# Sums of one pair issued ahead of the masks of the next in quarter-array blocks, with an earlier A, an earlier O unit and a split weight load

## The chip, the cores and the metric

The kernel runs on one core of a Trainium2 chip (trn2). The metric is the device time of one execution in microseconds (us); the span in a profile is 1 to 2 us shorter, because it goes from the first to the last instruction.

Engine names: PE is TensorE (matmuls), PEld its weight loads, DVE is VectorE, ACT ScalarE, POOL GpSimd, SP SyncE. L316 is a line of the kernel. The changed kernel is seven lines longer from the state update on, so L388, L418, L442 of the kernel before are L395, L425, L449 after, and the mask line L352 is L351.

## The reference

Linear attention with a decaying state (batch 4, 8 heads, 768 steps, head size 64), then a feed-forward layer whose activation is h·cos(h):

```python
for t in range(S):
    state = gamma * state + k[t] v[t]^T          # per batch and head
    y[t] = (1/sqrt(D)) * q[t] @ state
x = y, heads joined                               # 3072 x 512
h = x @ w_in                                      # 512 -> 2048
out = (h * cos(h)) @ w_out                        # 2048 -> 512
```

The kernel works on chunks. A "pair" is two batches of one chunk of 128 steps; there are twelve pairs, and two pairs form a group of 512 tokens. Per pair: **A** = keys times queries, **masks** (DVE, lower triangle), **sums** = masked A times values, **Y** = the state's part of y, **U** = the state update. **F** is a piece of the first feed-forward matmul, followed by a cosine on ACT and a product on DVE; **O** is a quarter of a 128-token tile of the second.

## The kernel before: the parts that matter

From pair 4 on, Y, A, U and the sums run as 64x64 matmuls, four at a time in quarters of the PE array. One block holds Y of pair p, A and U of pair p+1, then the masks of p+1, then the sums of p. Sums and A results share four PSUM banks: sums in columns 0-255, A in columns 256-511.

```python
def block(py=None, pa=None, pu=None, split=False):
    yb = {(u, r): banks.take() for u in range(2) for r in range(2)}
    ...                                   # Y of py -> yb[..][:, :256]; A of pa -> yb[..][:, 256:]
    ...                                   # U of pu -> two more banks
    if py is not None and not split:
        order = nc.sync.nop(nofuse=True)  # SP passes on that A has ended
        tc.add_manual_dep(order.ins, last.ins.name, SYNC, reason="sums in order")
    if pa is not None:
        for b in range(2):
            for r in range(2):
                masked = nc.vector.tensor_tensor(out=am[pa % 2][r][:, b],
                    in0=yb[b, r][:, 256:]..., in1=mask..., op=ALU.mult)
                order = order or masked
    def sums():
        ...                               # 32 matmuls into yb[u, b][:, :256], b outermost
        ...                               # four ACT copies of yb[u, b][:, :256] into xt
        ...                               # give the four banks back
    ...
    elif not split:
        sums()                            # with split, the caller issues them one slot later
```

The start, where the first weights come in, and the stretch between the early and the steady stage:

```python
load(nc.gpsimd, 1, ("q0", "k0", "q1", "k1"))
load_w_in(0)                              # columns 0-511, 1 MB in HBM
load(nc.gpsimd, 1, ("v0", "v1"))
...
m1 = stage_a(1, (0,)); masks(1, m1)
later = []
pair_f(0, 0, (0,), later)                 # first F: needs columns 0-255
m1 = stage_a(1, (1,)); masks(1, m1)
conv_v_plain(1, 0); conv_v_plain(1, 1)    # ACT
pair_f(0, 0, (1,), later)
...
stage_y(1, nc.scalar.copy)
...
pair_f(1, 0)                              # first F of pair 1: needs both xt copies
...
plan[1] = [(0, "c", 5), (1, "t", 4), (3, "a", 4), (4, "c", 6), (6, "t", 5), (8, "B", 4),
           (10, "c", 7), (13, "Y", 5)]    # (slot, what, pair): c casts and loads, t transposes
for g in range(1, NG + 1):
    for s in range(16):
        if 1 < g < NG: unit_f(g, s)
        unit_o(g - 1, *divmod(s, 4))
        ...                               # then what the plan has for slot s
```

Of the kernel before, what the change touches and what calls it, by code (L numbers as in the profile page):

```python
# [31 lines left out]
def kernel(  # L32
# [9 lines left out]
    nc = tc.nc  # L42
# [82 lines left out]
    def load_w_in(r, n=512):  # L125
        nc.gpsimd.dma_start(
            out=w_in_sb[:, :, ts(r, n)],
            in_=moe_w_in[:, ts(r, n)].rearrange("(i p) f -> p i f", p=128))
# [95 lines left out]
    def stage_a(p, bs=(0, 1)):  # L224
        n = p % NB
        todo = []
        for b in bs:
            bk = [banks.take(), banks.take()]
            ap = [t.rearrange("p (a t) -> p a t", a=HP) for t in bk]
            for a in range(HP):  # L230
                for j in range(2):
                    po = 64 * j
                    nc.tensor.matmul(ap[j][:, a, :], lhsT=kt(n, b, a)[po : po + 64, :],  # L233
                                     rhs=qt(n, b, a)[po : po + 64, :],
                                     tile_position=(po, 0))
            todo.append((b, bk, ap))
        return todo
# [67 lines left out]
    def block(py=None, pa=None, pu=None, split=False):  # L305


        started = set()
        yb = {}
        if py is not None or pa is not None:  # L310
            yb = {(u, r): banks.take() for u in range(2) for r in range(2)}

        def mm(bank, col, cols, row, lhsT, rhs):
            first = (id(bank), col) not in started
            started.add((id(bank), col))
            return nc.tensor.matmul(bank[half(col), cols], lhsT=lhsT, rhs=rhs, start=first,  # L316
                                    stop=True, skip_group_check=True,
                                    tile_position=(64 * row, 64 * col))

        if py is not None:  # L320
            n = py % NB
            for a in range(HP):
                for u in range(1 if py % NC == 0 else 0, 2):
                    st = stb[py % 2][:, 0] if u == 1 else stb[(py - 1) % 2][:, 1]
                    for b in range(2):
                        for i in range(2):
                            mm(yb[u, b], i ^ b, ts(a, 64), i, st[half(i), ts(4 * b + a, 64)],
                               qt(n, b, a)[half(i), half(u)])
        if pa is not None:
            n = pa % NB  # L330
            for b, a in BA:
                for u in range(2):
                    for i in range(2):
                        last = mm(yb[b, i ^ u], u, ts(4 + a, 64), i,
                                  kt(n, b, a)[half(i), half(u)], qt(n, b, a)[half(i), half(u)])
        ub = []
        if pu is not None:
            n = pu % NB
            ub = [banks.take() for _ in range(1 if pu % NC == NC - 1 else 2)]
            for b, a in BA:  # L340
                for i in range(2):
                    for u, bank in enumerate(ub):
                        mm(bank, i, ts(4 * b + a, 64), u, ks[n][half(u), b, 2 * a + i, :],
                           vs[n][half(u), b, 2 * a + (i ^ b), :])
        order = None
        if py is not None and not split:
            order = nc.sync.nop(nofuse=True)
            tc.add_manual_dep(order.ins, last.ins.name, SYNC, reason="sums in order")
        if pa is not None:
            for b in range(2):  # L350
                for r in range(2):  # L351
                    masked = nc.vector.tensor_tensor(  # L352
                        out=am[pa % 2][r][:, b],
                        in0=yb[b, r][:, 256:].rearrange("p (a t) -> p a t", a=HP),
                        in1=mask.unsqueeze(1).to_broadcast([128, HP, 64]), op=ALU.mult)
                    order = order or masked

        def sums():
            n = py % NB
            if order is None:  # L360
                nc.tensor.drain()
            for b, a in BA:
                for j in range(2):
                    for u in range(2):
                        m = mm(yb[u, b], j, ts(a, 64), u, vs[n][half(u), b, 2 * a + j, :],
                               am[py % 2][j ^ b ^ u][half(u), b, a, :])
                        if order is not None and b == a == j == u == 0:
                            tc.add_manual_dep(m.ins, order.ins.name, SYNC, reason="sums in order")
            for b in range(2):
                for u in range(2):  # L370
                    nc.scalar.copy(  # L371
                        out=xt[(py // 2) % 2].rearrange(
                            "p a (h b u t) -> p h b u a t", h=2, b=2, u=2)[:, py % 2, b, u],
                        in_=yb[u, b][:, :256].rearrange("p (a t) -> p a t", a=HP))
            for bank in yb.values():
                banks.give(bank)

        if py is None:
            for bank in yb.values():
                banks.give(bank)  # L380
        elif not split:
            sums()
        if pu is not None:
            for u, bank in enumerate(ub):
                if pu % NC == 0 and u == 0:
                    nc.vector.tensor_copy(out=stf[:, 0], in_=bank)
                else:
                    nc.vector.tensor_tensor(out=stf[:, u], in0=bank, in1=stf[:, 1 - u],  # L388
                                            op=ALU.add)
                banks.give(bank)  # L390
                nc.scalar.copy(out=stb[pu % 2][:, u], in_=stf[:, u])  # L391
        return sums
# [29 lines left out]
    def pair_f(p, r, parts=(0, 1), later=None):  # L422

        g, hf = divmod(p, 2)
        for f in [4 * r + 2 * i for i in parts]:  # L425
            bank = banks.take()
            for e in range(2):
                for i in range(KIN):
                    nc.tensor.matmul(bank[:, ts(e, 256)], lhsT=w_in_sb[:, i, ts(f + e, 128)],  # L429
                                     rhs=xt[g % 2][:, i, ts(hf, 256)],  # L430
                                     start=(i == 0 and e == 0), stop=(i == KIN - 1),
                                     skip_group_check=True)
            act(bank, gt[g % 2][:, f : f + 2, ts(hf, 256)], later)
# [33 lines left out]
    def masks(p, items):  # L467
        for it in items:
            stage_m(p, it)

    load(nc.gpsimd, 1, ("q0", "k0", "q1", "k1"))
    load_w_in(0)
    load(nc.gpsimd, 1, ("v0", "v1"))
    conv_q(1, nc.gpsimd, (1,))
    load_w_in(1)
# [30 lines left out]
    stage_t(1, None, (1,))  # L506
    m1 = stage_a(1, (0,))
    masks(1, m1)
    later = []
    pair_f(0, 0, (0,), later)  # L510
    m1 = stage_a(1, (1,))
    masks(1, m1)
    conv_v_plain(1, 0)
    conv_v_plain(1, 1)
    pair_f(0, 0, (1,), later)
# [38 lines left out]
    masks(3, m3)  # L554
    pair_f(2, 2, (1,))
    pair_f(2, 3, (0,))
    stage_y(3, nc.scalar.copy)
    pair_f(2, 3, (1,))
    pair_f(3, 0)
    pair_f(3, 1)  # L560
    conv_k(4)
# [13 lines left out]
    sums = None  # L575
    for g in range(1, NG + 1):
        for s in range(16):
            if 1 < g < NG:
                unit_f(g, s)
            unit_o(g - 1, *divmod(s, 4))  # L580
            if sums is not None:
                sums()
                sums = None
            for at, what, p in plan.get(g, ()):
                if at != s or p >= NP:
                    continue
                if what == "t":
                    stage_t(p, False)
                elif what == "c":
                    if p > 5:  # L590
                        conv_q(p, nc.vector if g == 1 else nc.gpsimd)
                    conv_k(p)
                    if p >= PT:
                        stage_t_dma(p)
                    conv_v(p, nc.gpsimd)
                    if p + 2 < NP:
                        load(nc.sync, p + 2, ("q", "v0"))
                        load(nc.gpsimd, p + 2, ("k", "v1"))
                elif what == "a":
                    block(pa=p, pu=p)  # L600
                elif what == "b":
                    block(py=p, pa=p + 1, pu=p + 1)
                elif what == "B":
                    sums = block(py=p, pa=p + 1, pu=p + 1, split=True)
                else:
                    sums = block(py=p, split=True)
# [30 lines left out]
```

## Time and profile before

Three runs gave 222.04, 222.47 and 226.68 us. PE is the limit: it is busy 93% of the span, so I expected that only its idle time could be won (the result shows that this was too narrow). These lines are from the page of the kernel before: the span, PE's busy time, the granted PE clock in 40 slices (tenths of full speed), and the group of the 27 masks that read a plain bank (busy us, mean ns, then idle of DVE before them).

```profile
span 220.0 us, 5315 instructions
...
PE 204.7 (93%) x2214; PEld 112.8 (51%) x2236; DVE 112.5 (51%) x194; ACT 125.4 (57%) x218; POOL 83.2 (38%) x93
...
PEclk9996999999999999999999999999999999999998
...
L352 DVE TENSOR_TENSOR am<-bank,mask 128x256 bf16<-128x256 f32 x27 | 9.9, 415 | 3.3 <-PE bank L316 3.3
```

The clock row is full except in one slice (16.5 to 22 us) and in the last, after the last matmul. The next fence is the time line of one block, at 121 us (start, duration, engine, line, operation, count; the U matmuls are left out).

```profile
121.07 0.44 PE L316 MATMUL bank<-qkt,stb 64*64 64x64 bf16 x32
...
121.34 0.44 PE L316 MATMUL bank<-qkt 64*64 64x64 bf16 x32
...
121.74 1.42 DVE L352 TENSOR_TENSOR am<-bank,mask 128x256 bf16<-128x256 f32 x4
...
122.22 0.19 PE L316 MATMUL bank<-am,vs 64*64 64x64 bf16 x1
...
122.88 0.65 PE L316 MATMUL bank<-am,vs 64*64 64x64 bf16 x31 [0.48 <-DVE am L352]
...
123.07 0.68 DVE L388 TENSOR_TENSOR stf<-bank,stf 128x512 f32<-128x512 f32 x1
123.23 1.20 ACT L371 CAST xt<-bank 128x256 bf16<-128x256 f32 x4 [2.23 <-PE bank L316]
```

A ends at 121.78, the U matmuls at 122.10. The sums (`bank<-am,vs`) start at 122.22 and end at 123.53: the first stands alone, right after the first mask, and the other 31 come 0.66 us later, right after the third mask. The list of waits of PE sums this up as follows (total us, times, longest):

```profile
PE bank L316 <- DVE am L352: 2.4, 6, 0.5
```

At the start PE idles from 15.82 to 17.24 us for the first weights. In the windows below (length, then busy us of PE, PEld, DVE, ACT, POOL, then the clock as a share of full speed, the DMA share and GB/s) PE does nothing from 16 to 17 us, and has half its clock after that:

```profile
16.00:17.00 1.00, 0.00 (x0) 0.00 (x0) 1.00 (x3) 0.45 (x1) 0.89 (x2) 0.95 1.07 215
17.00:18.00 1.00, 0.76 (x4) 0.58 (x5) 0.23 (x1) 0.00 (x0) 0.52 (x1) 0.50 1.19 201
...
19.00:20.00 1.00, 1.00 (x11) 0.63 (x11) 0.22 (x1) 0.77 (x2) 0.14 (x2) 0.50 1.19 193
20.00:21.00 1.00, 0.98 (x8) 0.79 (x7) 1.00 (x3) 0.94 (x2) 0.90 (x1) 0.84 1.27 210
```

### The profile page before, as it was taken

What the parts mean: (1) busy time and instruction counts of PE and PEld (TensorE: products, weight loads), DVE (VectorE), ACT (ScalarE), POOL (GpSimd) and SP (SyncE); (2) the same over time, 40 slices, a digit from 0 to 9 for tenths busy, and PEclk for the clock granted to TensorE, in tenths of its full rate; (3) what the DMA queues carried; (4) which work ended last, traced back from release to release, by engine and by line L of the source; (5) the groups of instructions that cost most, each with busy time, mean ns of one, the idle gap of its engine ahead of it and who ended that gap; (6) DMA issues with size and microseconds to landing.
All of it is one profiled execution on the core that took longest, in us unless ns stands there. A gap on an engine that the chain in (4) does not pass through costs nothing.

```text
span 220.0 us, 5315 instructions
## 1 busy us (share of the span) xinstructions
PE 204.7 (93%) x2214; PEld 112.8 (51%) x2236; DVE 112.5 (51%) x194; ACT 125.4 (57%) x218; POOL 83.2 (38%) x93
## 2 busy tenths in 40 slices
PE   7878999999999999999899899899899999999992
PEld 2445878878755444444544544544444444444440
DVE  4685498697569227654643644544544244433000
ACT  5564887867957644685565565664544644454120
POOL 7995679964999737370703300000000000000000
PEclk9996999999999999999999999999999999999998
DMA  6999999999677999979865531441011011110221
GB/s 157 301 205 221 284 317 240 197 254 344 193 261 168 265 309 203 297 114 258 167 119 170 51 95 48 55 95 48 4 48 48 3 49 48 51 48 0 95 81 62
DMA packets 43256, 32.85 MB, mean 149 GB/s; under 512 B 32480, under 2 KB 36832, under 8 KB 43232
## 3 DMA queue, kind: packets, MB, share of 16 engines
q0 software_dynamic: 8320, 18.35, 32.7%
q1 hardware_dynamic: 34768, 14.03, 27.9%
q8 instruction: 17, 0.28, 0.5%
q10 hardware_dynamic: 144, 0.13, 0.2%
q14 instruction: 7, 0.06, 0.1%
HBM read 27.26 MB, written 6.29 MB: 153 GB/s over the span
## 4 chain that ended last, share of the span: by engine, by line
PE 75%; DVE 8%; ACT 5%; DMA 4%; POOL 3%; issue 3%; DVEq 0%; POOLq 0%
PE bank L442 30%; PE bank L418 21%; PE bank L429 10%; DMA w_in_sb<-in_moe_w_in_dram 4%; PE st_ps L418 4%; PE st_ps L442 3%; PE bank L316 3%; DVE am L352 3%; DVE gt L407 2%; ACT cosb L400 2%; POOL kf L120 1%; DVE am L242 1%; PE bank L203 1%; ACT ks L186 1%; ACT qkt L207 1%
## 5 line engine op out<-in xcount | busy, mean ns | idle before, releaser
L407 DVE TENSOR_TENSOR gt<-bank,cosb 128x512 bf16<-128x512 f32 x86 | 58.0, 689 | 68.5 <-ACT cosb L400 68.5
L442 PE MATMUL bank<-w_out_sb,gt 128*128 128x512 bf16 x345 | 85.4, 379 | 0.7 <-issue 0.5
L400 ACT ACTIVATE cosb<-bank,halfpi 128x512 bf16<-128x512 f32 x86 | 58.2, 690 | 42.1 <-PE bank L418 33.1
L442 PEld LDWEIGHTS <-gt 128*128 128x128 bf16 x384 | 37.1, 98 | 43.6
L418 PE MATMUL bank<-xt,w_in_sb 128*128 128x512 bf16 x210 | 55.1, 379 | 1.1 <-issue 0.6
L418 PEld LDWEIGHTS <-w_in_sb 128*128 128x128 bf16 x256 | 24.4, 98 | 29.0 <-issue 0.5
L429 PE MATMUL bank<-xt,w_in_sb 128*128 128x256 bf16 x248 | 29.9, 279 | 1.9 <-DMA w_in_sb<-in_moe_w_in_dram 1.4
L429 PEld LDWEIGHTS <-w_in_sb 128*128 128x128 bf16 x256 | 25.0, 100 | 5.7 <-DMA w_in_sb<-in_moe_w_in_dram 1.6
L181 POOL TENSOR_TENSOR vs<-vf,gk 128x512 bf16<-128x512 f32 x20 | 21.4, 1093 | 10.8 <-PE bank L316 8.3
L176 POOL TENSOR_TENSOR qs<-qf,gq 128x512 bf16<-128x512 f32 x15 | 15.4, 1044 | 24.5 <-issue 7.4
L454 ACT COPY ob<-bank 128x512 f32<-128x512 f32 x21 | 12.5, 594 | 10.7 <-PE bank L442 10.6
L120 POOL DMA_DIRECT2D vf<-in_v_dram x16 | 15.0, 938 | 3.5 <-DMA w_in_sb<-in_moe_w_in_dram 2.6
L120 POOL DMA_DIRECT2D kf<-in_k_dram x15 | 15.8, 1054 | 1.0 <-DMA w_in_sb<-in_moe_w_in_dram 0.6
L371 ACT CAST xt<-bank 128x256 bf16<-128x256 f32 x28 | 8.7, 383 | 12.8 <-PE bank L316 12.8
L407 DVE TENSOR_TENSOR gt<-st_ps,cosb 128x512 bf16<-128x512 f32 x10 | 6.9, 690 | 10.3 <-ACT cosb L400 10.2
L242 DVE TENSOR_TENSOR am<-bank,mask 128x512 bf16<-128x512 f32 x16 | 10.1, 682 | 3.5 <-PE bank L233 3.5
L391 ACT CAST stb<-stf 128x512 bf16<-128x512 f32 x14 | 8.4, 639 | 5.7 <-DVE stf L388 3.7
L352 DVE TENSOR_TENSOR am<-bank,mask 128x256 bf16<-128x256 f32 x27 | 9.9, 415 | 3.3 <-PE bank L316 3.3
L186 ACT CAST ks<-kf 128x512 bf16<-128x512 f32 x20 | 11.5, 630 | 0.0
L207 ACT COPY qkt<-bank 128x1024 bf16<-128x1024 bf16 x8 | 7.9, 1012 | 5.6 <-PE bank L203 5.6
L400 ACT ACTIVATE cosb<-st_ps,halfpi 128x512 bf16<-128x512 f32 x10 | 6.9, 691 | 7.0 <-PE st_ps L418 6.9
L176 DVE TENSOR_TENSOR qs<-qf,gq 128x512 bf16<-128x512 f32 x9 | 10.0, 1136 | 1.4 <-DMA qf<-in_q_dram 1.4
(69 smaller groups left out, 157.5 us busy)
## 6 DMA issues: line engine op xcount, KB each, us to landing
out_dram<-ob SPq DMA_DIRECT2D x23, 256.0 KB, 2.0
kf<-in_k_dram POOLq DMA_DIRECT2D x8, 512.0 KB, 6.8
vf<-in_v_dram POOLq DMA_DIRECT2D x13, 256.0 KB, 7.0
qf<-in_q_dram SPq DMA_DIRECT2D x5, 512.0 KB, 5.9
w_in_sb<-in_moe_w_in_dram POOLq DMA_DIRECT2D x4, 512.0 KB, 10.1
w_out_sb<-in_moe_w_out_dram POOLq DMA_DIRECT2D x4, 512.0 KB, 9.1
kf<-in_k_dram POOLq DMA_DIRECT2D x7, 256.0 KB, 7.3
qf<-in_q_dram POOLq DMA_DIRECT2D x6, 256.0 KB, 7.6
```

The source lines that it names most:

```text
L120: eng.dma_start(out=t[p % PRE][:, bs].rearrange("p b h d -> p (b h) d"), in_=src[2 * bp : 2 * bp + 2, :, ds(c * C, C)][bs].rearrange("b h ...
L176: eng.tensor_tensor(out=slots(p, qs[p % NB], b), in0=pairs(qf[p % PRE][:, b]), in1=pairs(bc(gq, p % NC)), op=ALU.mult)
L181: eng.tensor_tensor(out=vs[p % NB][:, b], in0=vf[p % PRE][:, b], in1=bc(gk, p % NC), op=ALU.mult)
L186: nc.scalar.copy(out=slots(p, ks[p % NB], b), in_=pairs(kf[p % PRE][:, b]))
L242: nc.vector.tensor_tensor(out=am1[p % 2][b][j], in0=ap[j], in1=mask1.unsqueeze(1).to_broadcast([128, HP, 128]), op=ALU.mult)
L352: masked = nc.vector.tensor_tensor(out=am[pa % 2][r][:, b], in0=yb[b, r][:, 256:].rearrange("p (a t) -> p a t", a=HP), in1=mask.unsqueeze( ...
L400: nc.scalar.activation(out=cb, in_=bank, func=AF.Sin, bias=halfpi)
L407: nc.vector.tensor_tensor(out=out, in0=h, in1=cb, op=ALU.mult)
L418: nc.tensor.matmul(bank, lhsT=w_in_sb[:, i, ts(f, 128)], rhs=xt[g % 2][:, i, :], start=(i == 0), stop=(i == KIN - 1))
L429: nc.tensor.matmul(bank[:, ts(e, 256)], lhsT=w_in_sb[:, i, ts(f + e, 128)], rhs=xt[g % 2][:, i, ts(hf, 256)], start=(i == 0 and e == 0), s ...
L442: nc.tensor.matmul(bank, lhsT=gt[g % 2][:, f, ts(j, 128)], rhs=w_out_sb[:, f, :], start=(f == 0), stop=(f == KOUT - 1))
L454: nc.scalar.copy(out=o, in_=bank)
```

## The change

Its intent is to take waits off PE: sums no longer wait for masks, PE fills its wait for the first weights with A of pair 1, the first weights come in two halves, an F piece and an O unit fill the waits around Y of pair 3, and one of the two copies of transposed data of pairs 4 and 5 goes to DVE.

```diff
@@ block
-        if py is not None and not split:
-            order = nc.sync.nop(nofuse=True)
-            tc.add_manual_dep(order.ins, last.ins.name, SYNC, reason="sums in order")
-        if pa is not None:
+        def masks():
+            first = None
             for b in range(2):
                 for r in range(2):
                     masked = ...
+            return first
...
+        if split:
+            order = masks() if pa is not None else None
+        elif py is not None:
+            order = nc.sync.nop(nofuse=True)
+            tc.add_manual_dep(order.ins, last.ins.name, SYNC, reason="sums in order")
+            sums()
+        if not split:
+            if pa is not None:
+                masks()
             for bank in yb.values():
                 banks.give(bank)
...
@@ start
-    load_w_in(0)
+    load_w_in(0, 256)
+    load_w_in(1, 256)
...
+    m1 = stage_a(1, (1,))
+    masks(1, m1)
     later = []
     pair_f(0, 0, (0,), later)
-    m1 = stage_a(1, (1,))
-    masks(1, m1)
@@ pair 3
     pair_f(2, 3, (0,))
+    pair_f(2, 3, (1,))
     stage_y(3, nc.scalar.copy)
-    pair_f(2, 3, (1,))
+    unit_o(0, 0, 0)
     pair_f(3, 0)
@@ loop
-            unit_o(g - 1, *divmod(s, 4))
+            if (g, s) != (1, 0):
+                unit_o(g - 1, *divmod(s, 4))
...
-                    stage_t(p, False)
+                    stage_t(p, True)
```

More of the change, by code (lines that the diff above doesn't have):

```diff
@@ L355, in block @@
                         in1=mask.unsqueeze(1).to_broadcast([128, HP, 64]), op=ALU.mult)
-                    order = order or masked
+                    first = first or masked
+            return first
         def sums():
@@ L374, in sums @@
                         in_=yb[u, b][:, :256].rearrange("p (a t) -> p a t", a=HP))
+            if split:
+                for bank in yb.values():
+                    banks.give(bank)
+        if split:
+            order = masks() if pa is not None else None
[6 more added lines that the diff above has]
+                masks()
             for bank in yb.values():
                 banks.give(bank)
-        if py is None:
-            for bank in yb.values():
-                banks.give(bank)
-        elif not split:
-            sums()
         if pu is not None:
```

## The prediction

> **What bounds the kernel now.** TensorE: the page shows PE busy 204.7 of 220.0 us (93%), and the chain of waits is 75% PE. The change adds almost no work, so it can only win PE's idle time. By windows: 0-20 us 4.2 us idle, 20-60 us 1.5, 60-80 us 1.1, 80-160 us 4.0, then almost none until the tail.
>
> **Steady stage (largest term).** Five blocks (near 92, 105, 121, 138, 154 us) have sums of one pair and masks of the next. Timeline at 121 us: the U matmuls end at 122.10; the first sum starts at 122.22, after mask 1 (ends 122.16); the second at 122.88, after mask 3 (122.84); sums end 123.53; the next F starts at 123.68. Masks read and sums write the same PSUM banks at other columns. The Trainium skill, "PSUM — Partial Sum Buffer", section "PSUM bank collisions raise a hardware error", says to guard PSUM by bank, not by address; the trace agrees: a sum waits for its bank's mask. With sums first they run from 122.15 to 122.8: 0.7 us a block. At 92 us the first sum waits for SP (93.18), held by an output DMA: 0.5 there. Sum 3.3 us. The masks (1.4 us), state additions and casts come 1 to 2 us later; DVE (51%) and ACT (57%) are not the limit and the results are wanted eight slots (14 us) later, so nothing is given back.
>
> **Start.** PE idles 15.8-17.24 us for the first 512 weight columns; A of pair 1, second half, is ready at 16.04 but queued behind. After: A at 16.1-16.6, the first 256 columns near 16, F from 16.6. The granted clock is 0.5 from 17 to 20.3 us; it may stay higher. But F of pair 1 waits for both xt copies, on ACT behind the v conversions and a cosine, and the second v of pair 1 lands at 19.98. Estimate: conversions end 20.65 instead of 20.95, F at 22.6 instead of 23.14. The extra weight DMA costs POOL 0.77 us of issue. Gain 0.5 us (0 to 1.2).
>
> **Pair 3.** Its Y waits 48.34-48.93 for the last mask. An F piece (0.87 us) ahead covers this; the O unit (0.86 us) covers the xt copies. Gain 0.45 us.
>
> **Pairs 4, 5.** One of two transposed copies moves from ACT (1.0 us) to DVE (0.69). Block 4/5 now waits for ACT until 68.81, gap 0.28 us. Risk: on DVE the copy stands behind the pair 6 q conversions (one took 3.09 us beside POOL's multiplies). Gain 0.3 us (-0.6 to 0.5).
>
> **Predicted time.** Gain about 4.5 us from fast runs near 222.3: 217.9 us, range 216.3 to 220.0. Chances: faster by over 2% 0.50, within 2% 0.48, slower 0.02.
>
> **What would show it.** In the five blocks no wait of sums for masks (now 2.4 us in six waits), masks after sums, first stb matmul to next F 1.9 instead of 2.6 us; slots still 1.73 us. F before 17 us; F of pair 1 at 22-22.8. No idle inside Y of pair 3. Group 2's first F near 76.1 instead of 77.33; the lead grows from 1.2 us there to 4.5 at 160 us.
>
> **What would make it wrong.** Sums wait for the ordering semaphore through SP longer than the U matmuls hide; xt copies on ACT and masks on DVE exclude each other on a bank, so late casts hold up cosines and F runs out of banks; DVE's late copy stalls block 4/5; v or later weights land later because of the split DMA; the clock gate falls otherwise.

## The result, and the profile after

Four runs gave 214.80 to 215.40 us, median 215.06, against a median of 222.47 for the fast runs of the kernel before until then (222.04, 222.47 and 222.55; the fourth, 226.68, is slow). The ratio is 0.9673 (95% interval 0.9647 to 0.9698). All ratios here are the mean time of one kernel's fast runs over that of the other's of the same rounds, so not quite the ratio of the medians that I quote. Executions over 1.5% slower than the fastest of the same kernel are left out of the means. That is 7.4 us off by the medians, where I had predicted 4.5, and it lies below my range (216.3 to 220.0). The page of the changed kernel:

```profile
span 213.1 us, 5296 instructions
...
PE 201.1 (94%) x2213; PEld 111.2 (52%) x2236; DVE 112.1 (53%) x196; ACT 123.6 (58%) x216; POOL 84.1 (39%) x94
...
PEclk9999999999999999999999999999999999999998
...
L351 DVE TENSOR_TENSOR am<-bank,mask 128x256 bf16<-128x256 f32 x27 | 10.3, 418 | 9.4 <-ACT xt L371 5.1
```

The clock row no longer has the gap. The mask group now waits for ACT's xt copies. The same block after (the U matmuls again left out):

```profile
117.67 0.45 PE L316 MATMUL bank<-qkt,stb 64*64 64x64 bf16 x32
...
117.94 0.44 PE L316 MATMUL bank<-qkt 64*64 64x64 bf16 x32
...
118.52 0.45 PE L316 MATMUL bank<-am,vs 64*64 64x64 bf16 x32
...
118.89 1.20 ACT L371 CAST xt<-bank 128x256 bf16<-128x256 f32 x4 [1.29 <-PE bank L316]
...
118.90 1.04 PE L425 MATMUL bank<-xt,w_in_sb 128*128 128x512 bf16 x3
...
119.29 1.64 DVE L351 TENSOR_TENSOR am<-bank,mask 128x256 bf16<-128x256 f32 x4 [0.97 <-ACT xt L371]
...
120.85 0.68 DVE L395 TENSOR_TENSOR stf<-bank,stf 128x512 f32<-128x512 f32 x1
```

All 32 sums now run in 0.45 us, with no break, and F follows at 118.90. Masks come last, each behind the xt copy of its bank. The whole block, first Y matmul to last sum, takes 118.97 - 117.67 = 1.30 us, where before it took 123.53 - 121.07 = 2.46.

To find where the 6.9 us between the two spans came from, I cut both traces at four events. "F of pair 1" is the start of the first F of that pair, "T of pair 4" that of its transposes, "full F" the first F of group 2, "last matmul" its end. All in us from the traces; the gain is the difference of the two columns.

| stretch | before | after | gain | predicted |
|---|---|---|---|---|
| start to F of pair 1 | 23.14 | 20.74 | 2.40 | 0.5 |
| F of pair 1 to T of pair 4 | 36.12 | 35.25 | 0.87 | 0.45 |
| T of pair 4 to first full F | 18.07 | 19.82 | -1.75 | 0.3 |
| first full F to last matmul | 138.67 | 133.33 | 5.34 | 3.3 |
| last matmul to end of span | 4.00 | 3.96 | 0.04 | 0 |

So no term was right: three gained more, and one lost where I expected a gain. The two pages also show that the gain was not idle time alone: PE's idle time fell by 3.3 us (15.3 to 12.0) and its busy time by 3.6 (204.7 to 201.1), since a matmul at half clock, and sums that trickle out behind masks, count as busy (in the block shown, 1.85 us busy before and 1.30 after). The loss has a clear place in the trace after. DVE's copy of pair 4 is done at 58.18 (first line). ACT (next two lines) waits until 58.26 for the keys of pair 5, and its own copy of pair 4 stands behind their casts, so A of pair 4 (PE, last line) starts only at 60.36 and waits for that copy:

```profile
57.50 0.68 DVE L205 COPY qkt<-bank 128x1024 bf16<-128x1024 bf16 x1
58.26 1.14 ACT L186 CAST ks<-kf 128x512 bf16<-128x512 f32 x2 [1.45 <-DMA kf<-in_k_dram]
...
59.30 1.00 ACT L207 COPY qkt<-bank 128x1024 bf16<-128x1024 bf16 x1
...
60.36 0.34 PE L316 MATMUL bank<-qkt 64*64 64x64 bf16 x17 [1.58 <-ACT qkt L207]
```

### The profile page after: what moved, and what is told of

Read it like the earlier page. It is cut to its first block, busy times and chain, and to the rows that moved or that the text cites. A ratio compares the mean times of both kernels' runs of the same rounds, so it can differ in the third digit from the quotient of the medians.

```text
span 213.1 us, 5296 instructions
## 1 busy us (share of the span) xinstructions
PE 201.1 (94%) x2213; PEld 111.2 (52%) x2236; DVE 112.1 (53%) x196; ACT 123.6 (58%) x216; POOL 84.1 (39%) x94
## 4 chain that ended last, share of the span: by engine, by line
PE 72%; DMA 12%; POOL 8%; ACT 3%; issue 2%; DVE 1%; SPq 0%; POOLq 0%; DVEq 0%; ACTq 0%
PE bank L449 32%; PE bank L425 22%; DMA vf<-in_v_dram 9%; PE bank L436 6%; PE bank L316 4%; PE st_ps L425 4%; PE st_ps L449 3%; DMA kf<-in_k_dram 3%; POOL qf L120 2%; POOL kf L120 2%; POOL vs L181 1%; POOL vf L120 1%; ACT cosb L407 1%; POOL w_in_sb L126 1%; PE bank L203 1%
## 5 line engine op out<-in xcount | busy, mean ns | idle before, releaser
L407 ACT ACTIVATE cosb<-bank,halfpi 128x512 bf16<-128x512 f32 x86 | 57.6, 687 | 33.2 <-PE bank L425 24.2
L436 PE MATMUL bank<-xt,w_in_sb 128*128 128x256 bf16 x248 | 28.6, 273 | 0.7 <-ACT xt L269 0.7
L471 PE MATMUL bank<-gt 128*128 128x512 bf16 x26 | 9.0, 489 | 1.5 <-DVE gt L141 1.3
L120 POOL DMA_DIRECT2D qf<-in_q_dram x9 | 8.9, 994 | 1.6 <-DMA w_in_sb<-in_moe_w_in_dram 1.6
```

The costliest lines, as they stand in the source:

```text
L120: eng.dma_start(out=t[p % PRE][:, bs].rearrange("p b h d -> p (b h) d"), in_=src[2 * bp : 2 * bp + 2, :, ds(c * C, C)][bs].rearrange("b h ...
L407: nc.scalar.activation(out=cb, in_=bank, func=AF.Sin, bias=halfpi)
L436: nc.tensor.matmul(bank[:, ts(e, 256)], lhsT=w_in_sb[:, i, ts(f + e, 128)], rhs=xt[g % 2][:, i, ts(hf, 256)], start=(i == 0 and e == 0), s ...
```

## The experiments

In each trace I read the same four stretches. They turned out to add up almost exactly, which makes them the main evidence. All values are us; "clock" is the mean granted clock of the profiled run. In every trace with 0.995 or more here the clock falls only after the last matmul, so these runs had the full clock throughout the work; the values of 0.992 or less come from a half clock earlier on. Run 11 has no row, because its profiled run was slow.

| kernel | to F of pair 1 | to T of pair 4 | to full F | to last matmul | clock |
|---|---|---|---|---|---|
| before | 23.14 | 36.12 | 18.07 | 138.67 | 0.988 |
| after | 20.74 | 35.25 | 19.82 | 133.33 | 0.997 |
| 1 sums first only | 23.62 | 36.12 | 18.06 | 133.33 | 0.988 |
| 2 both changes of the start | 21.59 | 36.12 | 19.32 | 138.70 | 0.996 |
| 3 split load only | 20.64 | 36.13 | 19.45 | 138.70 | 1.000 |
| 4 early A only | 21.91 | 36.12 | 18.07 | 138.69 | 1.000 |
| 5 pair 3 only | 22.00 | 35.25 | 19.28 | 139.07 | 1.000 |
| 6 after, copies on ACT | 21.13 | 35.25 | 19.64 | 133.33 | 1.000 |
| 7 after, key casts behind copies | 21.40 | 35.25 | 17.85 | 133.39 | 1.000 |
| 8 before, sums a slot later | 21.51 | 36.11 | 18.07 | 138.59 | 0.997 |
| 9 after again | 20.40 | 35.25 | 21.66 | 133.34 | 0.992 |
| 10 as 7, first block a slot later | 21.33 | 35.25 | 18.13 | 133.74 | 0.999 |
| 12 before, wait filled | 22.03 | 36.12 | 18.06 | 138.69 | 0.996 |
| 13 before, fewer fillers | 23.51 | 36.12 | 18.07 | 138.68 | 0.981 |
| 14 after, fewer fillers | 21.60 | 35.25 | 19.08 | 133.33 | 1.000 |
| 15 before, fillers moved | 21.75 | 36.12 | 18.07 | 138.70 | 0.996 |

### 1. Sums first, nothing else

The edit is the block part of the diff above; all else is as before.

> The kernel before with only the order inside the blocks changed. Theory 1 (the sums themselves take about 0.35 us and the rest of their 0.65 us in the trace of before was a further wait, for mask 4): each of the five blocks gains 1.1 to 1.2 us (0.9 in the first), in all 5.5 us, time about 217.0 us. Rival (my prediction: a block gains 0.7 us, the rest of the lead comes from the other parts): 3.3 us, about 219.2 us.

The fast runs were 215.26, 216.31 and 216.83 us against a median of 220.67 for the kernel before on that chip, ratio 0.9757 (0.9675 to 0.9839). The stretch from the first full F to the last matmul is 133.33 us, exactly that of the changed kernel and 5.34 below before. So the block order alone is worth 5.34 us in the trace, and theory 1 holds against my 3.3. In time, the two runs at full clock (215.26, 216.31) are 4.7 us below the four of the kernel before (mean 220.52).

### 2 to 4. The parts of the start

Edits: both start hunks of the diff (2), only `load_w_in(0, 256); load_w_in(1, 256)` (3), only A of pair 1 moved ahead (4).

> The kernel before with both changes of the start: the split weight load and A of pair 1 ahead. Theory 1: F of pair 1 starts near 20.7 us (23.1 before), but the lead of 2.4 us is lost again at A of pair 4, because the keys of pair 5 land at a time set by DMA (58.2 us) and their casts stand on ACT ahead of both transposed copies: A of pair 4 near 61.3 us, so only about 0.7 us is left at the end, time about 221.8. Rival: the lead is kept, about 220.1.

> The kernel before with only the first weight load in two halves. Theory 1 (the split makes the v of pair 1 land sooner): its second v lands near 18.5 us and not 20.0, F starts near 16.1 and the clock gate stays open; F of pair 1 near 21.5. Rival (v landed sooner for another reason, such as the order on PE): v lands at 20.0 and F of pair 1 starts no sooner than 22.3. Time within 1% of before in either case, by the loss at A of pair 4.

> The kernel before with only A of pair 1 ahead of the first F. Theory 1: first F still at 17.2 us, half clock from about 17 us on, second v of pair 1 lands at 20.0, F of pair 1 near 22.6 (0.5 us sooner). Rival: the order on PE alone keeps the clock up and brings v sooner; F of pair 1 near 21. Time within 0.5% of before either way.

In time all three stay within noise: ratios 0.9948 (0.987 to 1.0027), 0.9957 (0.9892 to 1.0022) and 0.9957 (0.9888 to 1.0027). In the traces F of pair 1 starts at 21.59, 20.64 and 21.91. The expectation for 2 missed by 0.9 us at that point. The split load alone got the earliest start: the first F at 16.02, and the second v of pair 1 landed 7.0 us after its issue at 11.38, at 18.40. In the trace of before it was issued at 10.72 and landed 8.6 us later, at 19.37. I had read 19.98 from the moment at which POOL went on with its next issue; that is not the landing. Over all traces the second v lands between 17.9 and 19.2 with the split, and between 18.5 and 20.5 without it, so the split brings it forward by 0.7 us on average (18.45 against 19.12), with a large spread. Run 4 met neither of its expectations: the half clock did not come, and F of pair 1 at 21.91 is no sooner than in the traces of the old start at full clock (21.51 to 22.03).

Runs 2 and 3 also show the give-back: the stretch from T of pair 4 to the full F grows from 18.07 to 19.32 and 19.45, as A of pair 4 waits for the keys of pair 5. In run 4, where T of pair 4 comes at 58.03 and these keys land in time, it stays at 18.07.

### 5. Pair 3 only

```diff
+    pair_f(2, 3, (1,))
     stage_y(3, nc.scalar.copy)
-    pair_f(2, 3, (1,))
+    unit_o(0, 0, 0)
```

> The kernel before with only the F piece ahead of Y of pair 3 and the O unit behind it. Theory 1 (Y of pair 3 lost about 0.85 us to masks, in several short waits of which the list of waits names only 0.38): transposes of pair 4 come 0.85 us sooner after F of pair 1 than in before (36.1 us there). A of pair 4 is then again held by the pair 5 keys, so that at the end less than 0.8 us is left. Rival (prediction): 0.45 us.

From F of pair 1 to T of pair 4 it took 35.25 us instead of 36.12: 0.87, not my 0.45. The ratio is 1.0028 (0.9952 to 1.0103), so nothing of it reaches the end: 19.28 instead of 18.07 in the next stretch. Its last stretch was also 0.4 us longer than in every other kernel with the old block; its list of waits has 0.2 us there for transposed keys from DMA that the kernel before doesn't have, and the rest stays open.

### 6. Both copies back on ACT

```diff
-                    stage_t(p, True)
+                    stage_t(p, False)
```

> The changed kernel with both transposed copies of pairs 4 and 5 back on ACT. Theory 1 (keys of pair 5 land near 58.2 us whatever PE does, and every ACT copy behind their casts delays A of pair 4): A of pair 4 near 61.3 us instead of 60.4, and time 0.9 to 1.0 us longer than the changed kernel, near 216. Rival (prediction: the copy on DVE is worth 0.3 us or costs, behind the q conversions): within 0.3 us of the changed kernel.

Theory 1 missed here. Median 215.40 us, ratio 0.9781 (0.9707 to 0.9855); T of pair 4 to the full F took 19.64 us against 19.82 with the copy on DVE. A of pair 4 has two halves; the first starts as soon as the first copy is there (60.23), and in this run the keys of pair 6 landed earlier (63.87 against 64.88), which may hide up to about 1 us. Moving the copy to DVE brought nothing that these runs can show, neither my +0.3 us nor the cost I had feared.

### 7. Key casts behind the copies

```diff
-    plan[1] = [(0, "c", 5), (1, "t", 4), (3, "a", 4), (4, "c", 6), (6, "t", 5), (8, "B", 4),
+    plan[1] = [(1, "t", 4), (1, "c", 5), (3, "a", 4), (6, "t", 5), (6, "c", 6), (8, "B", 4),
```

> The changed kernel with the key casts of pairs 5 and 6 issued behind the transposed copies of pairs 4 and 5. Theory 1 (in-order ACT held by the DMA of the keys is what takes back the lead): no wait before A of pair 4, A near 58.8 us; then POOL's q conversion of pair 5 (done near 62.6) bounds the next transposes; first full F near 74.9 instead of 75.8, time 0.9 us shorter than the changed kernel, near 214.2. Rival (the lead is lost to DMA for other reasons): no gain.

Runs from 213.10 to 213.59 us, ratio to before 0.9678 (0.9602 to 0.9754). The stretch fell from 19.82 to 17.85 us. These lines of ACT show it: the copy runs at 57.29, ahead of the casts, which still wait for the keys (A of pair 4 then started at 59.36).

```profile
57.29 1.01 ACT L207 COPY qkt<-bank 128x1024 bf16<-128x1024 bf16 x1
58.66 1.14 ACT L186 CAST ks<-kf 128x512 bf16<-128x512 f32 x2 [0.35 <-DMA kf<-in_k_dram]
```

So the loss was in-order ACT standing still for a DMA, with work for PE queued behind it. The keys of pair 5 were issued by POOL at 44.0 to 45.8 us and landed about 13 us later, at 56.9 to 58.8, in all traces of the two tables, however far PE had come.

### 8. Masks first, sums one slot later

```diff
-                    block(py=p, pa=p + 1, pu=p + 1)
+                    sums = block(py=p, pa=p + 1, pu=p + 1, split=True)
```

> The kernel before with masks still first in the five blocks, but their sums issued one slot later (behind the next F and O). Theory 1 (the loss was only the wait of sums for masks of the same bank, not the work or the order): the stretch from the first full F to the last matmul takes about 133.4 us, as in the changed kernel, instead of 138.7, total 5.3 us under before. Rival (masks ahead of sums cost PE in some other way, or holding four banks one slot longer stalls F): 135 us or more.

The rival held: ratio 1.0006 (0.9917 to 1.0094), and 138.59 us in the last stretch. No sum waits for a mask any more, but new waits stand in their place. PE's waits from 76 to 215 us in this run:

```profile
PE bank L418 <- ACT xt L371: 2.0, 2, 1.8
PE st_ps L418 <- ACT xt L371: 1.8, 1, 1.8
PE bank L442 <- DVE gt L407: 0.8, 1, 0.8
```

The sums' banks are needed by later F pieces, and they come free only after the xt copies. Those now stand on ACT behind the state casts, the key casts and a cosine (in the trace the sums end at 122.73 and the xt copies start at 125.15). The wait was removed and returned in another form. In the changed kernel the xt copies start as the sums end (118.89 against 118.97), and F waits for them only once, for 0.2 us.

### 9 to 12. The changed kernel again, two improvements, and a filled wait

Edits: none (9); run 7 with `max(s, 8)` for `max(s, 7)` in `plan[2]` (10); run 7 again (11); and in the kernel before (12):

```diff
     m1 = stage_a(1, (0,))
     masks(1, m1)
+    warm(6)
     later = []
```

> The changed kernel again, beside the kernel before on this chip. Theory 2 (the kernel before has two clock modes, 220.2 us with a mean clock of 0.996 or more and 222 to 223 us with 0.988; the change always gets the first): about 215.0 us with a clock of 0.995 or more in every run, and a gain of about 5.2 us over the runs of before with the full clock, 7.4 us only over those with 0.988. Rival: the gain of 7.4 us is the change's own in every clock mode.

> Key casts behind the copies, and the first combined block one slot later, so that its ordering wait on SP no longer stands behind an output DMA. Theory 1: the first block then takes as long as the others, 0.25 us saved over the kernel with the key casts moved alone: about 213.1 us. Rival: the other order of units costs as much: no gain.

> Key casts of pairs 5 and 6 behind the transposed copies, beside the changed kernel on the same chip: 1.3 to 1.6 us faster than it, about 213.4 us. Rival: under 0.5 us, the difference of the earlier runs lay in the chips.

> The kernel before with six idle matmuls on PE where it waits for the first weights (15.8 to 17.2 us), nothing else. Theory 2 (the idle stretch there is what lets the clock gate close): mean clock 0.995 or more in every fast run, about 220.0 us, and none of the runs near 222. Rival (the clock falls for another reason): about as many runs at 0.988 as the kernel before has, or a slower start.

Ratios to the kernel before on this chip: 0.9781 (0.9737 to 0.9826) for the changed kernel, 0.9706 (0.9681 to 0.9730) for run 10, 0.9718 (0.9693 to 0.9742) for run 11. The fast means are 215.31, 213.73 and 213.90 us. So moving the key casts is worth about 1.4 us beyond the change by all fast runs, and 1.0 us by those at full clock (0.995 or more: 214.77 against 213.80). Run 7 shows 1.97 us in its stretch of the trace. Taking the slot 8 block did nothing in addition: its ordering wait on SP went, but 0.6 us of waiting for transposed keys came in the next block. Run 11's profiled run took 418.68 us. PE alone was stretched: it was busy 410.9 of 417.0 us and its 128x512 matmuls took 678 ns and not 379, while ACT, DVE and POOL were busy about as long as in the profile after. Its page has no clock row, so the value 1.000 for it says nothing. Why it happened is open.

On this chip the kernel before had eight fast runs, all with a clock of 0.996 or more and (but for one of 222.08) at 219.55 to 220.50 us. The gain of the change is then about 5.0 us (220.3 - 215.3, means), not 7.4. The changed kernel had two runs of six at 0.992 and 216.4 us; the other four, 214.09 to 215.58, had 0.996 or more. With these four alone, full clock on both sides, the gain is 5.5 us (220.29 - 214.77). The profile of one of the two, run 9, shows half clock after the wait for the keys:

```profile
58.00:60.00 2.00, 0.43 (x2) 0.00 (x0) 0.55 (x1) 1.45 (x3) 2.00 (x3) 1.00 0.46 74
60.00:62.00 2.00, 1.35 (x66) 0.94 (x67) 0.92 (x3) 1.08 (x2) 1.99 (x3) 0.80 0.88 285
62.00:64.00 2.00, 2.00 (x6) 0.70 (x5) 1.87 (x5) 0.66 (x2) 2.00 (x4) 0.50 0.87 231
64.00:66.00 2.00, 2.00 (x16) 1.06 (x15) 2.00 (x2) 0.92 (x2) 2.00 (x3) 0.85 0.88 314
```

PE stood idle from 58.43 to 60.65, the half clock came at 61.18, and the stretch to the full F took 21.66 us instead of 19.82. So theory 2 was right about the kernel before and wrong in that the changed kernel always keeps the clock. Run 12 had 0.996 or more in all six runs, at 220.07 to 221.60 us, but so had its neighbour without the filler: that experiment told nothing.

### 13 to 15. Provoking the clock

Edits: `warm(5)` and `warm(2)` around the second Y of pair 0 removed from the kernel before (13) and from the changed kernel (14); and removed from before with `warm(6)` added as in run 12 (15).

> The kernel before without the seven filler matmuls that it has on PE at 11 to 13 us. Theory 2 (the clock gate closes after a stretch of little PE activity, and the wait for the first weights at 15.8 to 17.2 us completes such a stretch): the half clock after the first weights comes in most runs, mean clock 0.988 or less, about 222.5 us. Rival (the half clock of some runs of before is chance, or the chip's): no more such runs than the kernel before has, about 220.2 us.

> The changed kernel without the same seven fillers. Theory 2 with the change as protection (A and F of pair 1 run from 15.8 us on, so the stretch is short): the clock holds at the start in most runs, about 215.3 us, apart from those that fall at the later wait near 59 us (216.4). Rival (the change does not protect, its runs were lucky): the start falls to half clock as often as in the kernel before without the fillers, about 217 us.

> The kernel before without the seven fillers at 11 to 13 us, but with six at 15.8 to 17.2 us. Theory 2: filling the wait itself keeps the clock, about 220.3 us at 0.995 or more in every fast run. Rival: what counts is the stretch at 11 to 13 us, and the clock falls as in the kernel without any of them.

Clocks of the fast runs: 0.981, 0.990, 0.980 and 1.000 (13, 220.87 to 222.29 us); 1.000, 0.992, 0.981 and 0.984 (14, 214.86 to 215.90); 0.996, 0.989, 0.996, 0.992 and 0.990 (15, 220.33 to 221.60). The kernel before had three of eight fast runs at 0.991 or less here (222.09 to 222.38), the other five at 219.96 to 221.18. So falls were seen in more of the runs without the fillers (three of four in run 13 against three of eight, three of four in run 14 against two of six in run 9, on another chip), but these counts are too small to show that the fillers matter. The change is no protection by itself, and filling the wait alone is none either. In the trace of run 13 the half clock sets in near 14 us, after the stretch with few matmuls at 12 to 14, and not at the wait for the weights:

```profile
12.00:14.00 2.00, 0.78 (x11) 0.44 (x10) 2.00 (x3) 0.59 (x1) 1.94 (x3) 0.98 1.12 189
14.00:16.00 2.00, 1.91 (x28) 1.62 (x28) 0.64 (x2) 1.26 (x2) 2.00 (x4) 0.50 1.14 288
...
18.00:20.00 2.00, 2.00 (x16) 1.14 (x15) 0.23 (x1) 0.49 (x1) 1.78 (x3) 0.50 1.13 171
20.00:22.00 2.00, 1.95 (x19) 1.28 (x21) 1.89 (x3) 1.84 (x4) 0.54 (x1) 0.81 1.21 205
```

What the traces show is that stretches of low activity come before the half clock; which of them is hit varies from run to run. In the 3.41 us before the half clock set in, PE was busy for 1.95 us (before, from 13.49), 1.19 (run 1, from 15.30), 1.19 (run 9, from 57.77) and 1.55 (run 13, from 10.53). But low activity alone does not decide: in the trace after it was busy for 1.67 of the 3.41 us from 58.10, and the clock stayed full.

## Why the prediction was wrong

**Steady stage: right mechanism, a term mis-sized.** I wrote "With sums first they run from 122.15 to 122.8: 0.7 us a block". That took the 0.65 us in which 31 sums ran as their own duration. After the change 32 sums take 0.45 us by the records. In the old time there was one more wait of 0.2 us, for the fourth mask: in the block at 92 us the second half of the sums starts at 94.06, 0.21 us after the one before it, and the masks end at 94.01 (92.60 + 1.41). The sums also used to start 0.12 us after the last U, and now start 0.15 us before its end. A block gained 1.15 us (0.74 in the first, held by SP as predicted), 5.34 in all instead of 3.3. The list of waits names only 2.4 us because it counts an idle PE, not matmuls that come slower than they could. "Nothing is given back" held here: masks end 1.2 us later against the block's start (1.6 in the first block), and run 1 and the changed kernel both take 133.33 us.

**The bank rule.** The Trainium skill, "PSUM — Partial Sum Buffer", section "PSUM bank collisions raise a hardware error", says that ACT's and DVE's reads of one bank must not overlap either. In the trace the program keeps them apart: five masks wait 5.1 us in all for xt copies. No run here shows what an overlap would do. I had named this as a risk that would starve F of banks; in the changed kernel it did no harm, and in run 8, where the copies come later, waits for banks and for what stood behind them (4.6 us in the list) took the gain.

**Start: a wrong wait, and no number for the clock.** "The second v of pair 1 lands at 19.98" was POOL's wake-up; it landed at 19.37. Nor did it hold F of pair 1 there. The conversions of v stood on ACT behind the first cosine, and this waited for the first F. These lines show the cosine and the two conversions, two lines before and two after:

```profile
19.23 0.69 ACT L400 ACTIVATE cosb<-bank,halfpi 128x512 bf16<-128x512 f32 x1 [2.78 <-PE bank L429]
19.82 1.13 ACT L194 CAST vs<-vf 128x512 bf16<-128x512 f32 x2
...
17.27 0.69 ACT L407 ACTIVATE cosb<-bank,halfpi 128x512 bf16<-128x512 f32 x1 [1.72 <-PE bank L436]
17.86 1.27 ACT L194 CAST vs<-vf 128x512 bf16<-128x512 f32 x2
```

Before, the first F ran from 17.24 to 19.13, at half clock; after, from 16.13 to 17.18 at full clock, and only now does v hold the second conversion (landing 18.49, conversion 18.52). Run 3, with F at 16.02, shows that the split load brings the first F forward; run 4, with the early A alone, has it at 17.45.

And "it may stay higher" put no number on the clock. With full clock, the old start brought F of pair 1 at 21.51 to 22.03 us (runs 5, 8 and 12, mean 21.85), the changed start at 20.40 to 21.59 (after, 2, 6, 7, 9, 10, mean 21.10): 0.75 us, near my 0.5, though the two ranges overlap. With half clock the old start took 23.14 to 23.62 (before, 1, 13; in run 1 v also landed late, at 20.47, and held its conversion). So roughly 1.3 of the 2.40 us (23.14 - 21.85) came from the clock mode of the kernel before in its first profile. Its fast runs there took 221.71 to 222.55 us; beside the experiments, on three chips, 20 of its 28 fast runs took 219.45 to 221.18 us.

**Pair 3: right mechanism, mis-sized.** 0.87 us and not 0.45; I had again taken the named wait (0.38 us) with little more than itself. Run 5 has it alone.

**Pairs 4 and 5: wrong step.** "Gain 0.3 us" became a loss of 1.75. I looked at the engines' order and not at what is timed from outside: the keys of pair 5 land near 58 us in any case, so a lead gained earlier turned into waiting there (A of pair 4 waited 1.58 us for a copy behind their casts). Runs 2, 3 and 5 show a loss of 1.2 to 1.4 us there without the copy on DVE, run 6 shows that the copy has no visible part in it, and run 7 removes it.

**Sum.** 2.40 + 0.87 - 1.75 + 5.34 + 0.04 = 6.90 us, the difference of the spans. The range missed it because the three errors upward (start 1.9, blocks 2.04, pair 3 0.42 us) outweighed the one downward (2.05). With full clock on both sides the same change gains about 5.5 us, not far from the 4.5 that I had predicted; that agreement is partly luck, since blocks and pairs 4 and 5 erred in opposite directions.

**What stays open.** What precisely brings the half clock in a given run, and why the split load lands v sooner although it is issued later.

## What to carry to other kernels

Time a stretch of work that waits on several events against the same work where it doesn't wait: a list of waits gives only a lower bound. When you free an engine, look for what is timed by DMA behind an in-order queue further on, and put casts of late data behind the copies that the critical engine wants; here that was worth a further 1.0 us beyond the change (runs at full clock; 1.4 by all fast runs). Compare kernels within one clock mode before you assign a gain to an edit.

## What the Trainium skill lacked or had wrong

- "TensorE: Matmul & The Clock Gate", section "Why this matters for your kernels", asks for no PE gaps above about 3 us to keep the clock. Here the half clock set in within a gap of 1.4 us (before, at 16.9 in the gap from 15.82 to 17.24) and 0.5 us after one of 2.2 us (run 9), but not after one of 1.6 us (the trace after, before 60.36). The length of a half-clock stretch, about 3.4 us (16.9 to 20.3 in before), fits the window that the page states in "Part 1: The HAM clock gate (the "warmup" mystery)", as does the variation from run to run.
- The same page, section "Wait — 56ns, not 53.3ns?", says that matmuls never start closer than about 25 ns. As that section words it, without an exception for matmuls in different quarters of the array, this is too wide: 32 of them here took 0.45 us from the first start to the last end, the last itself 0.19: about 8 ns from start to start.
- "PSUM — Partial Sum Buffer" gives the rule of guarding by bank, but no page says what a chain of such guards costs: 32 sums of 0.45 us were stretched to 1.31 us (122.22 to 123.53) by their waits for masks.
- "DMA: Bandwidth & Descriptors", section "Anatomy of one DMA — SWDGE (gpsimd) path", gives a fit per DMA and none for DMAs in a queue: for a 512 KB load an estimate from its formula is 3.2 us. Queued behind others on POOL the key loads at 41 to 46 us took 11.3 to 14.0 us to land.
